# First batch's heads all in fp32, the first head's bias by a matmul with ones, and conversions of two weights ordered by a ramp

## The chip, the cores and the metric

One core of a Trainium2 chip runs the program. The metric is the device time of one execution in microseconds (us). The engines: TensorE (PE; PEld is its weight load), VectorE (DVE), ScalarE (ACT), GpSimd (POOL), and SyncE (SP), whose queue issues every DMA here.

## The reference

```python
# attention: 4 batches, 8 heads, 576 rows, 64 columns
scores = q @ k.T / 8
cum = cumsum(maximum(s, 0))
bias = minimum(-(cum[:, None] - cum[None, :]), 0)
scores = where(causal, -1e9, scores + bias)
attn = exp(scores - max(scores)); attn /= sum(attn) + 1e-9
x = attn @ v                      # heads side by side: 2304 x 512
# two feed-forward parts
c = (x @ w1) * (x @ w2)           # 2304 x 1024
x2 = c @ w3 @ w_out               # 2304 x 512
h = x2 @ w_in                     # 2304 x 2048
out = (h - tanh(h)) @ w_out2      # 2304 x 512
```

The inputs q, k, v and s are fp32. The weights are float64, and the kernel reads their bits.

## The kernel before, in words

The order of the work is not that of the code. Every step is first written down as an operation with its engines, an estimated duration, the buffers that it reads and writes, and a priority (lower goes first). A planner (class `Plan`) then runs a list scheduling over these estimates and emits the instructions in the order that comes out; each engine works through its own list in that order. The numbers of `PARAM` set priorities and costs. Head number n has the priority 100n, products of the first feed-forward part have 1.0e6 and go where TensorE would otherwise wait. Where nothing is there for TensorE in the first 150 us, the planner puts in fillers: matmuls of `msk` into bank 2 (line 499), whose result nobody reads.

A head has five query tiles, 64, 128, 128, 128 and 128 rows, in two groups (tiles 0 to 2, and 3 and 4). For batch 0 the first groups of the eight heads come first (heads 0 to 7 in the numbering), then the second groups (8 to 15), then batch 1 in the same way (16 to 31). For a tile TensorE computes the scores with the bias, `red` on VectorE adds the mask and takes the row's extreme, ScalarE does exp (line 594), TensorE transposes (line 624), the result is copied to SBUF, and `pv` sums V (lines 659, or 661 and 664).

Heads come in two forms. In the full form q, k and the exp are plain fp32: one matmul for the scores (line 577), in which five rows under q and k (tile `rqk`) carry the bias, fetched by DMA from `rel`, the cumulative sums less the one in the middle of each tile; the transposed exp is copied into `en`. In the split form each fp32 operand becomes a high and a low part in a faster format by a copy and a subtraction (`split`): `qs`, `kh`, `kl`, `vs`, `eh`, `el`; the scores are two matmuls (lines 579 and 580), the sum of V two rows of them (661 and 664), and the halves are added on VectorE (line 671). All first groups of batch 0 and the second groups of its heads 0 and 1 are in the full form (`natb=2`), everything later in the split form.

For every pair of heads TensorE transposes the row sums (line 603), VectorE inverts them (604, 605), two DMAs bring them through DRAM into `xr`, and the pair's output is multiplied by it (697) and split into `xh` and `xl` for the products (line 723).

Weights pass through `assemble`: a DMA of the float64 bits, one step on ScalarE (431), four on VectorE (432 to 437), and then a split. For w1 and w2 there are sixteen such conversions of 128x512, eight for each half of the columns, with two priorities for the halves.

Of the kernel before, what the change touches and what calls it, by code (L numbers as in the profile page):

```python
# [16 lines left out]
P = 128  # L17
B, H, S, D = 4, 8, 576, 64
NH = B * H
# [18 lines left out]
PARAM = dict(byf=(0,), dsub=1000.0, dsub0=1000.0, dcopy=1000.0, dcopy0=600.0, dother=1000.0, dother0=1000.0, spi=500.0, lay=6, lay0=4, layp=2.2e5, layf=2.95e5, gate=0, dve0=1000.0, early=100.0e3, raw0=0, rawp=-700.0, ng=3, nosb=2, cut=(1,), convq=1200.0, natb=2, abk=1, wap=0.95e6, dve=1000.0, act=0.0, pool=0.0, sem=160.0, pesem=180.0, slow=1.1, convp=790.0, npre=4,  # L38
# [227 lines left out]
def tile_kernel(ctx, tc, qk, v, s, w1, w2, w3t, w_out, w_in, w_out2, out):  # L266
# [80 lines left out]
    def pe(cost, fn, r, w, prio):  # L347
        pl.op([("PE", cost, fn)], r=r, w=w, prio=prio)
# [114 lines left out]
    def values():  # L463
        m = nc.vector.memset
        m(fix.t[:NH], 1.0)
        m(fix.t[D:D + 5], 1.0)
        for R in rqk:
            m(R.t[D:D + 32, S:], 0.0)
        m(const.t[:, 0:1], SQ_B)
        m(const.t[:, 1:2], -T2)  # L470
        m(ssum.t, 1.0)
        m(msk.t[:, D:], 0.0)
        for e in e2:
            for t in range(5):
                if EW[t] > QT[t][1]:
                    m(e.t[:, EOFF[t] + QT[t][1]:EOFF[t] + EW[t]], 0.0)
            m(e.t[D:, EOFF[0]:EOFF[0] + D], 0.0)
        for x, o in ((eh, EB), (el, EB), (en, 0)):
            m(x.t[D:, o + 1024:].bitcast(F32), 0.0)
    pl.op([("DVE", 2700.0, values)], w=[const, ssum, (msk, 1), eh, el, en, fix] + [(R, 1) for R in rqk] + e2, prio=-2900)  # L480

    def patterns():
        make_identity(nc, ident.t)
        nc.gpsimd.affine_select(fix.t[D:D + 5], fix.t[D:D + 5], [[1, S]], ALU.is_ge, 0.0, D, -P)
        nc.gpsimd.affine_select(fix.t[D:D + 5], fix.t[D:D + 5], [[-1, S]], ALU.is_ge, 0.0, P - 1 - D, P)
        nc.gpsimd.affine_select(msk.t[:, 448:], msk.t[:, 448:], [[-1, P]], ALU.is_ge, MASKED8, 0, 1)
    pl.op([("POOL", 3000.0, patterns)], w=[ident, (fix, 1), (msk, 1)], prio=-2500)
# [19 lines left out]
    dve(lambda: nc.vector.tensor_tensor_scan(rel.t[2 * NH:, :S], fix.t[:NH], rel.t[:NH, :S], 0.0, op0=ALU.mult, op1=ALU.add), S, [(rel, 0), (fix, 0)], [(rel, 5)], -1000)  # L507
# [24 lines left out]
    def head(h, full, groups=(0, 1)):  # L532
        b, hh = divmod(h, H)
        i = n_head[0] % 2
# [10 lines left out]
        if not full:  # L545
            dma(lambda: KL.t[D:D + 10, :qb].bitcast(F32), lambda: kb_d.t[h, :, :, :qb].rearrange("n t s -> (n t) s"), 10 * qb * 4, [kb_d], [(KL, 1)], pr - 245)
        else:
            for t0, t1 in ((0, 3), (3, 5)) if 1 in groups else ((0, 3),):
                a, o = ROFF[t0]
                dma(lambda t0=t0, t1=t1: R.t[D + t0:D + t1, S:S + qb],  # L550
                    lambda t0=t0, t1=t1, a=a: rel.t[a + h:a + h + 1, :(t1 - t0) * S].rearrange("p (t s) -> p t s", s=S)[:, :, :qb],
                    (t1 - t0) * qb * 4, [(rel, range(t0, t1))], [(R, 1)], pr - 245)
# [12 lines left out]
        def softmax_tile(t):  # L565
# [5 lines left out]
            for n, (k0, k1) in enumerate(pieces):  # L571
                bk = s_ring.next()

                def mm(bk=bk, k0=k0, k1=k1):
                    o_ = bk.t[:nq, :k1 - k0]
                    if full:
# [4 lines left out]
                if full:  # L581
                    pe(c_pe4(k1 - k0), mm, [R], [bk], p_)
                else:
                    pe(2 * c_pe(k1 - k0, nq), mm, [Q, Q2, KH, KL], [bk], p_)
# [154 lines left out]
    for half in range(2):  # L739
        for k in range(KC):  # L740
            for src, hb, lb in ((w1, w1h, w1l), (w2, w2h, w2l)):
# [3 lines left out]
                        PARAM["convp"] + half * PARAM["convq"], PARAM["rawp"] if half == 0 and 2 * k + (src is w2) < PARAM["raw0"] else None)  # L745
# [194 lines left out]
```

## Time and profile before

| | us |
|---|---|
| median of 3 runs | 985.87 |
| lowest, highest | 984.68, 987.29 |
| the profiled execution | 984.61 |
| its span | 982.9 |
| TensorE busy in the span | 955.8 |
| VectorE, ScalarE, GpSimd busy | 721.6, 603.7, 400.1 |

The profile is of one execution, and the span is what lies between its first and last instruction. A busy TensorE includes the fillers and the drain of its matmuls. The clock of TensorE is given as a share of 2.4 GHz.

### The profile page before, as it was taken

Reading aid. Unit: us, or ns where it says so; the run is one execution under the profiler, and the core shown is the slowest. Engines: PE = TensorE matmul, PEld = TensorE weight load, DVE = VectorE, ACT = ScalarE, POOL = GpSimd, SP = SyncE. Lnnn points to the kernel's source line nnn. Section 1 sums busy time; section 2 is a strip of 40 time slices with the busy share of each in tenths; the row PEclk is TensorE's granted clock in tenths of the full one; section 3 lists DMA queues with packets and bytes.
Section 4 is the critical chain, followed back from the end, with each engine's and each line's share of the span. In section 5 each row is a group of like instructions: output and inputs, shape, how many; then the busy total and the mean of one; then the engine's idle time right before and its main releaser. Section 6 shows DMA issues by size and latency. Waiting matters only on the chain.

```text
span 982.9 us, 16588 instructions
## 1 busy us (share of the span) xinstructions
PE 955.8 (97%) x5650; PEld 835.4 (85%) x5650; DVE 721.6 (73%) x1449; ACT 603.7 (61%) x1379; POOL 400.1 (41%) x341
## 2 busy tenths in 40 slices
PE   7989799999999999999999999999999999999998
PEld 6568699999999999888988898878888888888897
DVE  7879998788988959996786988985445455454454
ACT  4777867788878854443454447665455555654565
POOL 2346675654554434442254637442222222222222
PEclk7999899999999999999999999999999999999999
DMA  5667537645545315558679773103003000200010
GB/s 171 186 192 229 146 86 234 190 138 174 162 140 181 103 39 160 179 166 277 203 269 325 247 245 141 44 26 125 1 1 107 22 1 1 87 1 0 1 44 22
DMA packets 70092, 124.45 MB, mean 127 GB/s; under 512 B 6780, under 2 KB 39172, under 8 KB 70008
## 3 DMA queue, kind: packets, MB, share of 16 engines
q1 hardware_dynamic: 70008, 123.41, 39.3%
q8 instruction: 44, 0.72, 0.3%
q14 instruction: 40, 0.33, 0.1%
HBM read 93.34 MB, written 25.99 MB: 121 GB/s over the span
## 4 chain that ended last, share of the span: by engine, by line
PE 82%; DVE 7%; DMA 5%; issue 2%; ACT 2%; POOL 1%; SPq 0%; DVEq 0%; POOLq 0%; ACTq 0%
PE bank L865 19%; PE bank L723 16%; PE bank L888 6%; PE bank L886 6%; PE bank L887 6%; PE bank L624 4%; PE bank L828 3%; PE bank L827 3%; PE bank L829 3%; PE bank L661 2%; PE bank L664 2%; PE bank L579 2%; PE bank L580 2%; DMA xr<-r_d 2%; PE bank L791 1%
## 5 line engine op out<-in xcount | busy, mean ns | idle before, releaser
L334 POOL TENSOR_TENSOR gl<-pg,gh 128x512 fp32r<-128x512 f32 (+1 forms) x78 | 98.0, 1257 | 261.4 <-ACT gh L328 230.0
L865 PE MATMUL bank<-x2b,wih 128*128 128x512 f32 (+1 forms) x640 | 182.4, 370 | 0.0
L876 DVE TENSOR_TENSOR pg<-bank,u 128x512 f32<-128x512 f32 (+1 forms) x80 | 50.8, 635 | 142.3 <-ACT th L875 140.4
L865 PEld LDWEIGHTS bank<-x2b,wih 128*128 128x128 f32 x640 | 116.7, 188 | 21.7
L865 PE MATMUL bank<-x2b,wil 128*128 128x512 f32 (+1 forms) x320 | 117.9, 368 | 0.0
L888 PE MATMUL bank<-voh,gl 128*128 128x512 f32 x288 | 113.1, 393 | 0.4 <-POOL gl L334 0.3
L886 PE MATMUL bank<-voh,gh 128*128 128x512 f32 x288 | 113.0, 392 | 0.2 <-ACT gh L328 0.2
L887 PE MATMUL bank<-vol,gh 128*128 128x512 f32 x288 | 112.6, 391 | 0.0
L328 ACT ACTIVATE gh<-pg 128x512 fp32r<-128x512 f32 (+1 forms) x80 | 47.1, 589 | 87.2 <-DVE pg L880 85.7
L594 ACT ACTIVATE e<-e,nmx 64x64 f32<-64x64 f32 (+4 forms) x160 | 88.7, 556 | 12.3 <-DVE nmx L588 11.5
L873 ACT ACTIVATE u<-bank 128x512 f32<-128x512 f32 (+1 forms) x80 | 44.3, 554 | 71.4 <-PE bank L865 65.5
L431 ACT ACTIVATE wt<-wraw 128x512 f32<-128x512 f32 x72 | 47.9, 671 | 60.1 <-DMA wraw<-w_out 17.0
L624 PE MATMUL bank<-ident,e 128*128 128x128 f32 (+1 forms) x480 | 80.8, 277 | 3.4 <-ACT e L594 1.4
L723 PE MATMUL bank<-xh,w2h 128*128 128x288 f32 x256 | 80.6, 315 | 1.4 <-DVE cst L731 1.4
L723 PE MATMUL bank<-xh,w1h 128*128 128x288 f32 x256 | 81.3, 318 | 0.6 <-ACT asb L328 0.3
L588 DVE CUSTOM_DVE_ANT_0 e<-bank,msk 64x64 f32<-64x64 f32 (+4 forms) x160 | 64.6, 416 | 20.1 <-PE bank L580 9.1
L723 PE MATMUL bank<-xl,w2h 128*128 128x288 f32 x256 | 75.7, 296 | 0.0
L723 PE MATMUL bank<-xh,w1l 128*128 128x288 f32 x256 | 75.7, 296 | 0.0
L723 PE MATMUL bank<-xl,w1h 128*128 128x288 f32 x256 | 75.6, 295 | 0.0
L723 PE MATMUL bank<-xh,w2l 128*128 128x288 f32 x256 | 75.5, 295 | 0.0
L332 DVE TENSOR_TENSOR el<-bank,eh 128x512 fp32r<-128x512 f32 (+2 forms) x162 | 73.5, 474 | 2.5 <-ACT eh L328 2.0
L880 DVE COPY_PREDICATED pg<-mk,th 128x512 f32<-128x512 uint32 (+1 forms) x80 | 61.6, 770 | 12.5 <-ACT mk L878 5.1
(139 smaller groups left out, 2629.2 us busy)
## 6 DMA issues: line engine op xcount, KB each, us to landing
rqk<-qk SPq DMA_DIRECT2D x30, 576.0 KB
wraw<-w_out SPq DMA_DIRECT2D x24, 512.0 KB
c_d<-cst SPq DMA_DIRECT2D x32, 288.0 KB
wraw<-w SPq DMA_DIRECT2D x16, 512.0 KB
wraw<-w3t SPq DMA_DIRECT2D x16, 512.0 KB
cf<-c_d SPq DMA_DIRECT2D x32, 256.0 KB
wraw<-w_in SPq DMA_DIRECT2D x16, 512.0 KB
x_d<-x2s SPq DMA_DIRECT2D x16, 512.0 KB
```

The source lines that it names most:

```text
L332: o = [("DVE", c_dve(n), lambda: nc.vector.tensor_tensor(dst(), a(), b().bitcast(F32), op=ALU.subtract))]
L334: o.append(("POOL", c_pool2(n), lambda: nc.gpsimd.tensor_tensor(dst(), a(), b().bitcast(F32), op=ALU.subtract)))
L588: nc.vector.tensor_tensor_reduce(e.t[:nq, EOFF[t] + k0:EOFF[t] + k1], bk.t[:nq, :k1 - k0], bi.t[:nq, bo + k0:bo + k1], -0.125, 3.0e38 if f ...
L594: act(lambda: nc.scalar.activation(et(), et(), AF.Exp, bias=nmx.t[:nq, i, tm:tm + 1], scale=-1.0, accum_out=ssum.t[:nq, pj, t, i:i + 1]), ...
L624: nc.tensor.transpose(bk.t[:rows, n * P:(n + 1) * P], e.t[:, EOFF[t] + c * P:EOFF[t] + c * P + rows], ident.t)
L723: nc.tensor.matmul(bk.t[:, :HALF], w_.t[:, k, f * P:(f + 1) * P], x_.t[:, k, o:o + HALF], start=k == 0 and j == 0, stop=k == KC - 1 and j ...
L865: nc.tensor.matmul(bk.t[:, :w], w_.t[:, k, a], X2.t[:, i, k, :w], start=k == 0 and n == 0, stop=k == KC - 1 and n == 2)
L876: dve(lambda u=u, pg=pg, hp=hp, c_=c_: nc.vector.tensor_tensor(c_(pg), hp(), c_(u), op=ALU.mult), w, [bk, u], [pg], pr)
L880: dve(lambda pg=pg, mk=mk, th=th, c_=c_: nc.vector.copy_predicated(c_(pg), c_(mk).bitcast(U32), c_(th)), w, [mk, th], [pg], pr, two=True)
L886: nc.tensor.matmul(bank[n].t, gh.t[:, a], voh[f].t, start=f == 0, stop=False)
L887: nc.tensor.matmul(bank[n].t, gh.t[:, a], vol[f].t, start=False, stop=False)
L888: nc.tensor.matmul(bank[n].t, gl.t[:, a], voh[f].t, start=False, stop=f == NF2 - 1)
```

## The change

Three things are changed. First, `natb` goes from 2 to 8: the second groups of heads 2 to 7 of batch 0 take the full form too, and the pool with the second set of split buffers opens after all of them. Second, the very first group (head 0, tiles 0 to 2) takes its bias from `rel` by a second matmul, whose other operand, in unused columns of the second exp buffer, has a first row of ones and zeros below; its rows of the bias in `rqk` are no longer fetched. The constants are set in two steps, with those that the first heads need ahead of the scan, the others behind the row blocks, and GpSimd's patterns are three operations. Third, the priorities of the sixteen conversions: 790 for the first eight and 1990 for the others become ramps from 590 to 940 and from 1790 to 2140 in steps of 50 (`convp` 790 to 590, new `ramp0` and `ramp1` of 50.0). The table `PARAM` is left out below.

```diff
--- before.py
+++ after.py
...
@@ -465,9 +465,14 @@
         m(fix.t[:NH], 1.0)
         m(fix.t[D:D + 5], 1.0)
         for R in rqk:
-            m(R.t[D:D + 32, S:], 0.0)
-        m(const.t[:, 0:1], SQ_B)
-        m(const.t[:, 1:2], -T2)
+            m(R.t[D:D + 5, S:], 0.0)
+        m(sel(), 0.0)
+        m(sel()[0:1], 1.0)
+    sel = lambda: e2[1].t[:NH, EOFF[4]:EOFF[4] + P]
+    pl.op([("DVE", 2600.0, values)], w=[fix, (e2[1], 4)] + [(R, 1) for R in rqk], prio=-2900)
+
+    def more():
+        m = nc.vector.memset
         m(ssum.t, 1.0)
         m(msk.t[:, D:], 0.0)
         for e in e2:
@@ -475,16 +480,18 @@
                 if EW[t] > QT[t][1]:
                     m(e.t[:, EOFF[t] + QT[t][1]:EOFF[t] + EW[t]], 0.0)
             m(e.t[D:, EOFF[0]:EOFF[0] + D], 0.0)
+        m(const.t[:, 0:1], SQ_B)
+        m(const.t[:, 1:2], -T2)
         for x, o in ((eh, EB), (el, EB), (en, 0)):
             m(x.t[D:, o + 1024:].bitcast(F32), 0.0)
-    pl.op([("DVE", 2700.0, values)], w=[const, ssum, (msk, 1), eh, el, en, fix] + [(R, 1) for R in rqk] + e2, prio=-2900)
+    pl.op([("DVE", 1900.0, more)], w=[const, ssum, (msk, 1), eh, el, en] + [(e, range(4)) for e in e2], prio=-850)
 
     def patterns():
-        make_identity(nc, ident.t)
         nc.gpsimd.affine_select(fix.t[D:D + 5], fix.t[D:D + 5], [[1, S]], ALU.is_ge, 0.0, D, -P)
         nc.gpsimd.affine_select(fix.t[D:D + 5], fix.t[D:D + 5], [[-1, S]], ALU.is_ge, 0.0, P - 1 - D, P)
-        nc.gpsimd.affine_select(msk.t[:, 448:], msk.t[:, 448:], [[-1, P]], ALU.is_ge, MASKED8, 0, 1)
-    pl.op([("POOL", 3000.0, patterns)], w=[ident, (fix, 1), (msk, 1)], prio=-2500)
+    pl.op([("POOL", 1700.0, lambda: make_identity(nc, ident.t))], w=[ident], prio=-2600)
+    pl.op([("POOL", 1330.0, patterns)], w=[(fix, 1)], prio=-2500)
+    pl.op([("POOL", 400.0, lambda: nc.gpsimd.affine_select(msk.t[:, 448:], msk.t[:, 448:], [[-1, P]], ALU.is_ge, MASKED8, 0, 1))], w=[(msk, 1)], prio=-2400)
 
 
     def constants(i):
@@ -504,7 +511,7 @@
         dma(lambda i=i: rqk[i].t[D:D + 5, :S], lambda: fix.t[D:D + 5], 5 * S * 4, [(fix, 1)], [(rqk[i], 1)], -990)
     dma(lambda: rel.t[:NH, :S], lambda: s, NH * S * 4, [], [(rel, 0)], -1000)
     dve(lambda: nc.vector.tensor_scalar(rel.t[:NH, :S], rel.t[:NH, :S], 0.0, 8.0, op0=ALU.max, op1=ALU.mult), S, [(rel, 0)], [(rel, 0)], -1000, fast=True)
-    dve(lambda: nc.vector.tensor_tensor_scan(rel.t[2 * NH:, :S], fix.t[:NH], rel.t[:NH, :S], 0.0, op0=ALU.mult, op1=ALU.add), S, [(rel, 0), (fix, 0)], [(rel, 5)], -1000)
+    dve(lambda: nc.vector.tensor_tensor_scan(rel.t[2 * NH:, :S], fix.t[:NH], rel.t[:NH, :S], 0.0, op0=ALU.mult, op1=ALU.add), S, [(rel, 0), (fix, 0)], [(rel, 5)], -1000, extra=650.0)
 
 
     for t, (q0, q1) in enumerate(QT):
@@ -531,6 +538,7 @@
 
     def head(h, full, groups=(0, 1)):
         b, hh = divmod(h, H)
+        one = n_head[0] == 0
         i = n_head[0] % 2
         pj = n_head[0] // 2 % 2
         pr = n_head[0] * 100.0
@@ -544,7 +552,7 @@
             lambda: qk[h, :rows].rearrange("p (two s) -> p two s", two=2)[:, :, :qb], rows * 2 * qb * 4, [], [(R, 0)] if full else [R], pr - 250)
         if not full:
             dma(lambda: KL.t[D:D + 10, :qb].bitcast(F32), lambda: kb_d.t[h, :, :, :qb].rearrange("n t s -> (n t) s"), 10 * qb * 4, [kb_d], [(KL, 1)], pr - 245)
-        else:
+        elif n_head[0] > 1:
             for t0, t1 in ((0, 3), (3, 5)) if 1 in groups else ((0, 3),):
                 a, o = ROFF[t0]
                 dma(lambda t0=t0, t1=t1: R.t[D + t0:D + t1, S:S + qb],
@@ -573,12 +581,18 @@
 
                 def mm(bk=bk, k0=k0, k1=k1):
                     o_ = bk.t[:nq, :k1 - k0]
-                    if full:
+                    if one:
+                        a, o = ROFF[t]
+                        nc.tensor.matmul(o_, rq()[:D, q0:q1], rk()[:D, k0:k1], start=True, stop=False)
+                        nc.tensor.matmul(o_, sel()[:, :nq], rel.t[a:a + NH, o + k0:o + k1], start=False, stop=True)
+                    elif full:
                         nc.tensor.matmul(o_, rq()[:D + 5, q0:q1], rk()[:D + 5, k0:k1], start=True, stop=True)
                     else:
                         nc.tensor.matmul(o_, Q.t[:, q0:q1], KH.t[:, k0:k1], start=True, stop=False)
                         nc.tensor.matmul(o_, Q2.t[:NR, q0:q1], KL.t[:NR, k0:k1], start=False, stop=True)
-                if full:
+                if one:
+                    pe(2 * c_pe4(k1 - k0), mm, [(R, 0), (rel, t), (e2[1], 4)], [bk], p_)
+                elif full:
                     pe(c_pe4(k1 - k0), mm, [R], [bk], p_)
                 else:
                     pe(2 * c_pe(k1 - k0, nq), mm, [Q, Q2, KH, KL], [bk], p_)
@@ -742,7 +756,7 @@
                 convert(src[k * P:(k + 1) * P, half * 512:(half + 1) * 512],
                         lambda hb=hb, k=k, half=half: hb.t[:, k, half * 512:(half + 1) * 512], (hb, k * 2 + half),
                         lambda lb=lb, k=k, half=half: lb.t[:, k, half * 512:(half + 1) * 512], (lb, k * 2 + half),
-                        PARAM["convp"] + half * PARAM["convq"], PARAM["rawp"] if half == 0 and 2 * k + (src is w2) < PARAM["raw0"] else None)
+                        PARAM["convp"] + half * PARAM["convq"] + (2 * k + (src is w2)) * PARAM["ramp%d" % half], PARAM["rawp"] if half == 0 and 2 * k + (src is w2) < PARAM["raw0"] else None)
     raw_r.bufs, raw_r.i = raw, 0
     for h in range(H + 1):
         if h == PARAM["natb"]:
```

The places where the new order matters follow. VectorE's list at the start, before (the memset of `msk` and `fix` and of both `rqk` stand ahead; `rel` holds the cumulative sums):

```order
L471 MEMSET ssum 128x20
L472 MEMSET msk 128x512
L476 MEMSET e_115 128x64 x4
L477 MEMSET e_115 64x64
L476 MEMSET e_116 128x64 x4
L477 MEMSET e_116 64x64
L479 MEMSET eh 64x128
L479 MEMSET el 64x128
L479 MEMSET en 64x128
L506 TENSOR_SCALAR rel<-rel 32x576
L507 SCALAR_TENSOR_TENSOR rel<-fix,rel 32x576
L513 TENSOR_SCALAR rel<-rel 32x576 x5
```

and of the change, from the memset of `fix`:

```order
L466 MEMSET fix 5x576
L468 MEMSET rqk_105 5x576
L468 MEMSET rqk_106 5x576
L469 MEMSET e_116 32x128
L470 MEMSET e_116 1x128
L513 TENSOR_SCALAR rel<-rel 32x576
L514 SCALAR_TENSOR_TENSOR rel<-fix,rel 32x576
L520 TENSOR_SCALAR rel<-rel 32x576 x3
L476 MEMSET ssum 128x20
L477 MEMSET msk 128x512
```

The relu, the scan and three of the five row blocks now stand behind six short rows; the other memsets follow them.

TensorE's list in the second groups of batch 0, before, from the sum of V of head 2 on (`bank_60` takes the sum, `e` is the exp, `eh` and `el` its parts):

```order
L661 MATMUL bank_60<-eh,vs_114 128x256 x4
L661 MATMUL bank_60<-eh,vs_114 128x128
L664 MATMUL bank_60<-el,vs_114 64x256 x4
L664 MATMUL bank_60<-el,vs_114 64x128
L579 MATMUL bank_59<-kh_794,qs_793 128x288
L580 MATMUL bank_59<-kl_795,q_796 128x288
L624 MATMUL bank_61<-ident,e_116 128x128 x4
L579 MATMUL bank_58<-kh_111,qs_110 128x448
L580 MATMUL bank_58<-kl_112,q_113 128x448
```

and of the change, from the sum of V of head 0's second group on:

```order
L673 MATMUL bank_60<-en,rv_108 64x256 x4
L673 MATMUL bank_60<-en,rv_108 64x128
L638 MATMUL bank_63<-ident,e_116 128x128 x4
L737 MATMUL bank_65<-xh_89,w2h 128x288
L737 MATMUL bank_65<-xl_91,w2h 128x288
L737 MATMUL bank_65<-xh_89,w2l 128x288
L589 MATMUL bank_58<-rqk_105 128x448
L617 MATMUL bank_62<-ident,ssum 4x128
L638 MATMUL bank_61<-ident,e_116 128x128 x4
L589 MATMUL bank_59<-rqk_105 128x288
```

Each pair of split matmuls is one fp32 matmul now, for the scores and for the sum of V; products stand between them.

VectorE's list in the same part of the program, before:

```order
L329 CAST kh_111<-rqk_105 128x576
L332 TENSOR_TENSOR el<-bank_62,eh 128x4x128
L437 SCALAR_TENSOR_TENSOR wt_82<-wraw_81,wt_82 128x512
L731 TENSOR_TENSOR cst_131<-bank_65,asb_133 128x288
L332 TENSOR_TENSOR el<-bank_63,eh 64x128
L588 ISA e_116,nmx<-bank_59,msk 128x448
L588 ISA nmx 128x1
```

and of the change:

```order
L437 SCALAR_TENSOR_TENSOR wt_83<-wraw_107,wt_83 128x512
L329 CAST w1h<-wt_83 128x512
L432 TENSOR_SCALAR wt_88<-wt_88 128x512
L433 TENSOR_SCALAR wt_88<-wt_88 128x512
L435 SCALAR_TENSOR_TENSOR wt_88<-wraw_87,wt_88 128x512
L602 ISA e_116,nmx<-bank_59,msk 128x448
L602 ISA nmx 128x1
L602 ISA e_116,nmx<-bank_58,msk 128x288
```

The casts of k and the subtractions of `el` are gone, and steps of conversions stand between the reductions.

## Rows read from the trace of the kernel before

**Rows 1.** Busy time of each engine by stretch, TensorE's clock, DMA.

```profile
core 0: us, PE busy (x) PEld busy (x) DVE busy (x) ACT busy (x) POOL busy (x), PEclk, DMA share, GB/s
...
13.00:50.40 37.40, 35.63 (x193) 23.13 (x194) 29.09 (x86) 25.74 (x87) 12.57 (x12) 0.89 0.58 162
50.40:105.80 55.40, 46.95 (x353) 40.11 (x351) 47.66 (x112) 41.38 (x104) 31.78 (x34) 1.00 0.67 208
105.80:140.00 34.20, 31.75 (x230) 29.99 (x231) 31.91 (x79) 24.93 (x76) 23.98 (x26) 0.90 0.42 118
140.00:240.00 100.00, 99.78 (x790) 97.95 (x790) 83.06 (x238) 80.74 (x224) 53.37 (x55) 1.00 0.60 183
...
```

**Rows 2.** The same stretches, the fillers of line 499 alone.

```profile
13.00:50.40 37.40, 6.05 (x47) 4.91 (x47) 0.89 0.58 162
50.40:105.80 55.40, 5.44 (x58) 3.72 (x58) 1.00 0.67 208
105.80:140.00 34.20, 1.56 (x13) 0.92 (x13) 0.90 0.42 118
```

**Rows 3.** TensorE alone, in stretches of 2 us; the clock stands behind its count.

```profile
10.00:12.00 2.00, 0.00 (x0) 0.77 0.76 276
12.00:14.00 2.00, 0.98 (x4) 0.50 0.57 134
20.00:22.00 2.00, 2.00 (x9) 0.67 0.00 0
106.00:108.00 2.00, 1.25 (x8) 0.67 0.92 273
112.00:114.00 2.00, 2.00 (x12) 0.63 0.42 94
```

**Rows 4.** TensorE's timeline: start, time, line, operands, wait ahead with what ended it.

```profile
1.05 7.27 PE L499 MATMUL bank<-msk 128*128 128x128 bf16 x100 [1.05 <-DVE msk L495]
13.02 1.38 PE L577 MATMUL bank<-rqk 69*64 69x64 f32 x4 [4.69 <-DMA rqk<-rel]
...
48.83 1.40 PE L659 MATMUL bank<-en,rv 128*64 128x320 f32 x6 [0.65 <-ACT en L328]
...
50.43 0.27 PE L603 MATMUL bank<-ident,ssum 128*6 128x128 f32 x1
...
105.31 0.27 PE L603 MATMUL bank<-ident,ssum 128*4 128x128 f32 x1 [2.84 <-DVE el L332]
```

**Rows 5.** TensorE's timeline: scores and sums of V, in fp32 and split.

```profile
47.18 0.99 PE L577 MATMUL bank<-rqk 69*128 69x448 f32 x2
...
61.74 2.16 PE L659 MATMUL bank<-en,rv 128*64 128x256 f32 x10
...
100.76 0.77 PE L661 MATMUL bank<-eh,vs 128*128 128x256 f32 x5
101.37 0.69 PE L664 MATMUL bank<-el,vs 128*64 128x256 f32 x5
```

**Rows 6.** Timeline of VectorE and of SP's queue at the start.

```profile
2.35 1.15 DVE L468 MEMSET rqk<- 32x576 f32 x2
...
5.65 0.45 DVE L506 TENSOR_SCALAR rel<-rel 32x576 f32<-32x576 f32 x1
...
6.13 1.35 DVE L507 TENSOR_TENSOR_SCAN rel<-fix,rel 32x576 f32<-32x576 f32 x1
...
7.52 2.34 DVE L513 TENSOR_SCALAR rel<-rel 32x576 f32<-32x576 f32 x5
...
8.91 1.44 SPq L325 DMA_DIRECT2D rqk<-rel  x2
```

**Rows 7.** VectorE's groups by shape, 0 to 140 us: busy, mean ns, idle before.

```profile
L437 DVE SCALAR_TENSOR_TENSOR wt<-wraw,wt 128x512 uint32<-128x512 uint32 x16 | 14.1, 884 | 0.1
...
L332 DVE TENSOR_TENSOR el<-bank,eh 128x512 fp32r<-128x512 f32 x12 | 7.8, 680 | 0.4 <-ACT eh L328 0.4
...
L332 DVE TENSOR_TENSOR vs<-rv,vs 128x320 fp32r<-128x320 f32 x1 | 2.5, 2533 | 0.0
```

More of the change, by code (lines that the diff above doesn't have):

```diff
@@ L37 @@
 NR = D + 10
-PARAM = dict(byf=(0,), dsub=1000.0, dsub0=1000.0, dcopy=1000.0, dcopy0=600.0, dother=1000.0, dother0=1000.0, spi=500.0, lay=6, lay0=4, layp=2.2e5, layf=2.95e5, gate=0, dve0=1000.0, early=100.0e3, raw0=0, rawp=-700.0, ng=3, nosb=2, cut=(1,), convq=1200.0, natb=2, abk=1, wap=0.95e6, dve=1000.0, act=0.0, pool=0.0, sem=160.0, pesem=180.0, slow=1.1, convp=790.0, npre=4,
+PARAM = dict(ramp0=50.0, ramp1=50.0, byf=(0,), dsub=1000.0, dsub0=1000.0, dcopy=1000.0, dcopy0=600.0, dother=1000.0, dother0=1000.0, spi=500.0, lay=6, lay0=4, layp=2.2e5, layf=2.95e5, gate=0, dve0=1000.0, early=100.0e3, raw0=0, rawp=-700.0, ng=3, nosb=2, cut=(1,), convq=1200.0, natb=8, abk=1, wap=0.95e6, dve=1000.0, act=0.0, pool=0.0, sem=160.0, pesem=180.0, slow=1.1, convp=590.0, npre=4,
              nbias=3, keep=0.5, ff=0.0, fu=150.0e3, wlast=8, bw=370.0, ntr=3, actb=1, actn=0, spp=-80.0, ne=2, nsb=2, ncf=5, outlag=15)
```

## The prediction

> **What bounds the kernel now.** I read the profile from the end backwards. The table by stretches [rows 1] shows TensorE busy for 99.78 of the 100 us after 140 us. The stretches before it are another matter, so whatever the change is worth is decided ahead of 140 us: there I split TensorE's time into work and loss. Loss is idle time, the fillers on `msk` (matmuls whose result nobody reads) [rows 2], and half of the time in which TensorE works at the lower of its two clocks (1.2 instead of 2.4 GHz) [rows 3].
>
> - A, 0 to 13.0 us: 100 fillers, then a wait of 4.69 us until the first scores start at 13.02, ended by the DMA that writes rows of `rel` into `rqk` [rows 4]. All 13.0 us are loss.
> - B, 13.0 to 50.4, the first query groups of batch 0, up to the fourth transposition of row sums at 50.43 [rows 4]: 35.63 busy, less 6.05 of fillers, less about 4.2 because the clock is at its lower level from 11.1 to 21.3 us [rows 3]: 25.4 of work, 12.0 lost.
> - C, 50.4 to 105.8, the second query groups, up to the eighth such transposition at 105.31 [rows 4]: 46.95 less 5.44 makes 41.5 of work, 13.9 lost. VectorE is the busiest engine here, 47.66 of 55.4 us, a share of 0.86 [rows 1].
> - D, 105.8 to 140, the start of batch 1: 31.75 less 1.56, less about 3.4 for a lower clock from 106.7 to 113.5 [rows 3]: 26.8 of work, 7.4 lost.
>
> Together 46.3 us are lost. From then on TensorE has no gap worth naming, so the end is 984.61 (the profiled execution, 1.26 under the median of 985.87) less the loss that goes, plus the TensorE work that comes. Stages after 140 us get the same matmuls in nearly the same order, and I let them cancel.
>
> **The change part by part.**
>
> *TensorE work added.* Six heads of batch 0 now do their second group in full fp32. For the weighted sum of V the trace has both forms: five chunks, 1152 columns, take 2.16 us in fp32; split, 100.76 to 102.06, 1.30 us [rows 5]. That is 0.86 us more, 0.75 ns a column. The scores are 448 + 288 + 288 = 1024 columns, at the same rate 0.77 us more. Six heads: 9.8 us. The first head's bias by ones is a second fp32 matmul over 64 + 192 + 320 = 576 columns; at 2.16 us per 1152 columns, 1.1 us. Sum +10.9 us. From below the same numbers without the drain of the last matmul, from above the fp32 score row, 0.99 us for 448 columns [rows 5], 2.2 ns a column against 0.56: 10 to 14. I take 10.9, the nearer row in length.
>
> *Start (A).* The first head no longer waits for `rel` to pass through the DMA; its bias is read from `rel` by a matmul. On VectorE the order puts the memsets of `rqk` at the same place, ending 2.35 + 1.15 = 3.5 us [rows 6]; two small ones follow and then relu, scan and the first row block, where seventeen other memsets stood in between. 3.8 + 0.45 + 1.35 + 0.5 gives 6.1, against 8.0 before [rows 6], and the first matmul starts at about 6.3 if `s` has landed by 3.8; it has by 5.65, where relu ran without a wait for it, which makes 8.1 the other bound. Head 1 still goes through the DMA: issue at 8.91 and use at 13.02 are 4.1 us apart [rows 4, 6]. Three row blocks are done by 7.1, SP has one weight load fewer ahead, so the issue comes at 7.3 to 8.2 and head 1 at 11.4 to 12.5. Head 0's scores (2.2 us with the ones) and transposes lie inside that wait. I take 5 us less loss; from 2 (the late `s`, head 1 hardly earlier) to 6.5.
>
> *B.* The same instructions in other order, conversions a little later (six first steps on VectorE instead of eight before the fourth sums), and 74 fillers, beside the 28 in the wait for head 1, instead of 47 after the first scores. Fillers go where TensorE would wait, so they cost little: 0; from -1.5 to +2.7, the latter being 27 more fillers at the lower clock's 0.1 us each.
>
> *C.* Between the fourth and the eighth transposition VectorE loses its 19 subtractions (0.68 us for the common one [rows 7]), 4 casts and 4 additions, about 16 us, and gets five more conversions of four steps (a step is up to 0.88 us [rows 7]), 15 us. So VectorE stays near 47 while fourteen of the sixteen conversions are finished by the eighth transposition instead of twelve; ScalarE loses the copies that fed the splits, GpSimd the subtractions of q, k and v, and SP the 128-row loads, the `kb_d` reads and the copies of q. TensorE gets 9.8 us and gives 45 product matmuls away (57 instead of 102), 288 columns at the split rate, 0.14 us each, 6.3 us, which are done after C and are not lost. Its work becomes 45.0. The unknown is how well it can be packed: at VectorE's share of today, 0.86, C lasts 52.3 and loses 7.3; at TensorE's share of D, 31.75 of 34.2, 48.5 and 3.5; with all waits as they are, 13.9. I take 5.8, nearer to the first two, because the largest single wait there, 2.84 us, ends with a subtraction that no longer exists [rows 4].
>
> *D.* The lower clock from 106.7 follows that 2.84 us gap. With the gap gone I take 2 of the 3.4 us back, and 1.7 from VectorE, which starts one conversion here instead of four: 3.7 lost instead of 7.4; from 2 to 7.4. The buffers that odd heads of batch 1 need now open only when the last fp32 head is through; 48 products stand in TensorE's order between the eighth transposition and the first such head, and hide it.
>
> *The ramp.* It spreads the first eight conversions over heads 6 to 9 and the others over heads 18 to 21. It adds no instruction; its cost is in the counts used for B and C.
>
> One rule bears on this. Where VectorE and GpSimd overlap, the trace shows a 320-column subtraction in SBUF taking 2.53 us, while a 512-column one that reads PSUM takes 0.68 [rows 7]. The Trainium skill (SBUF — State Buffer, "SBUF: two separate sides") says that the two engines share one port pair as an exclusive lock, held for a whole instruction. By that rule GpSimd's lost subtractions would also shorten the conversions on VectorE, and C would pack as in the better bound.
>
> **Sum.** Loss 8.0 + 12.0 + 5.8 + 3.7 = 29.5 instead of 46.3: 16.8 less. Work +10.9. Net -5.9: 985.87 - 5.9 = 980.0 us.
>
> **Rivals.**
>
> 1. *TensorE takes VectorE's place and the waits stay.* Within a head the chain scores, reduction, exp, transposition, copy into `en`, sum of V is serial, and `en` has one buffer: the trace has a matmul on `en` that waited 0.65 us for ScalarE's copy [rows 4]. If that chain, now with fp32 matmuls in it, holds C at 13.9 and D at 7.4, only A gains: -5 + 10.9 = +5.9, 991.8. It decides where C and D together lose more than 15.4 us (break-even with A at 8; today 21.3, forecast 9.5), and the result is slower by over 0.3% beyond 18.4. For it: no filler or product stands in most of C's new order. Against it: the waits seen today in C end with subtractions and split loads that go.
> 2. *The start is only rearranged.* Only 30 fillers stand before the first scores and 28 after the second tile; while TensorE waited 4.69 us the clock fell, and it came back at 21.3 only [rows 3, 4]. If head 1 starts near 12.5 and the lower clock lasts some 5 us longer, A saves 2 and B loses 2.8 more: -2 + 2.8 - 8.1 - 3.7 + 10.9 = -0.1, 985.8. The Trainium skill (TensorE: Matmul & The Clock Gate, "HAM oscillation — how this bites in real kernels") says that idle gaps between bursts send the clock back to its lower level each time; the trace agrees, with 0.50 at 12 to 14 us after the gap of 4.69 us.
> 3. *Everything packs better.* C at 3.5, D at 2, A at 6.5: 24.0 instead of 46.3, -22.3 + 10.9 = -11.4, 974.5. The lock above would work this way. Against it: ScalarE, at 41.38 of 55.4 us in C [rows 1], is little relieved.
>
> **How the numbers follow.** Forecast 0.46, rival 1 0.15, rival 2 0.19, rival 3 0.20. A measurement of this kernel can tell about 0.3% (3 us) from no change. The forecast and rival 3 are faster by more, 0.66; rival 2 is within, 0.19; rival 1 is slower, 0.15. The likeliest time is 980.0. The low end takes all of rival 3 and what the bounds of A and B leave beyond it, 970; the high end reaches rival 1, 992. With the forecast alone the range would be 975 to 984.
>
> **What would show it.** First scores at 6 to 8 us and head 1 at 11.4 to 12.5; the fourth transposition of sums at about 45 us and the eighth near 96; a share of TensorE's busy time above 0.9 in that stretch with hardly any fillers; no lower clock at batch 1's start. The forecast is wrong if the eighth transposition comes after 102 us, or if TensorE shows new gaps after 140 us, which I let cancel.

## The result and the profile after

The changed kernel takes 976.95 us (median of 4 runs, 975.06 to 980.52) beside 986.58 of the kernel before: a ratio of 0.9894, 95% interval 0.9853 to 0.9935. In eight later runs beside 27 of before it was 980.57 us (974.85 to 982.94), 0.9922 with 0.9893 to 0.9951. So it is faster by 7.7 to 10.5 us by the ratios (6.5 to 9.6 by the medians). The forecast of 980.0 us, 5.9 less, had its sign right and was a little too small. One execution of all those reported here, 3314.4 us of the kernel without fillers, is left out as an outlier.

The table by stretches again, on the same events as [rows 1]: the fourth and the eighth transposition of sums end the second and the third stretch.

```profile
core 0: us, PE busy (x) PEld busy (x) DVE busy (x) ACT busy (x) POOL busy (x), PEclk, DMA share, GB/s
0.00:13.00 13.00, 10.59 (x69) 8.08 (x69) 9.28 (x36) 4.86 (x9) 3.92 (x11) 1.00 0.65 208
13.00:46.20 33.20, 31.44 (x219) 21.77 (x219) 26.25 (x74) 25.25 (x86) 12.59 (x12) 1.00 0.60 175
46.20:97.10 50.90, 50.34 (x299) 36.35 (x297) 44.76 (x103) 38.20 (x92) 23.23 (x23) 1.00 0.63 182
97.10:140.00 42.90, 40.79 (x320) 38.16 (x318) 31.83 (x96) 28.52 (x98) 25.08 (x31) 1.00 0.49 142
140.00:240.00 100.00, 99.44 (x792) 97.74 (x791) 86.38 (x245) 84.97 (x232) 55.21 (x58) 1.00 0.58 179
```

The fillers alone (line 506 now) in the same stretches, as [rows 2]:

```profile
0.00:13.00 13.00, 6.55 (x58) 6.02 (x58) 1.00 0.65 208
13.00:46.20 33.20, 7.24 (x74) 5.27 (x74) 1.00 0.60 175
46.20:97.10 50.90, 2.95 (x36) 2.43 (x36) 1.00 0.63 182
97.10:140.00 42.90, 1.46 (x12) 0.81 (x12) 1.00 0.49 142
```

In stretch C TensorE is busy for 50.34 of 50.90 us, 0.99, where it was 46.95 of 55.40 [rows 1]. Its lost time there is 0.56 idle and 2.95 of fillers: 3.5 us instead of 13.9. VectorE, the busiest engine before, stands at 0.88 behind it. The waits of TensorE from 46.2 to 140 us say the same; the 2.84 us of [rows 4] is gone, the longest is 1.1 and the three others that are listed are 0.5 each:

```profile
engine line waited for: us in total, times, longest us
PE bank L592 <- DMA r_d<-rinv: 1.1, 1, 1.1
```

TensorE's timeline at the start and at the three transpositions that mark the stretches, to be read beside [rows 4]:

```profile
1.05 3.38 PE L506 MATMUL bank<-msk 128*128 128x128 bf16 x30 [1.05 <-DVE msk L502]
4.46 0.47 PE L586 MATMUL bank<-rqk 64*64 64x64 f32 x2
6.26 0.47 PE L587 MATMUL bank<-rel,e 32*64 32x64 f32 x2 [1.34 <-DVE rel L520]
...
8.54 3.17 PE L506 MATMUL bank<-msk 128*128 128x128 bf16 x28
11.63 1.43 PE L586 MATMUL bank<-rqk 64*128 64x320 f32 x2
12.99 0.80 PE L587 MATMUL bank<-rel,e 32*128 32x320 f32 x2
...
14.56 0.85 PE L589 MATMUL bank<-rqk 69*64 69x64 f32 x4
...
20.65 0.27 PE L617 MATMUL bank<-ident,ssum 128*6 128x128 f32 x1
...
46.18 0.27 PE L617 MATMUL bank<-ident,ssum 128*6 128x128 f32 x1
...
97.11 0.27 PE L617 MATMUL bank<-ident,ssum 128*4 128x128 f32 x1
```

One thing here doesn't fit the clock column. The column reads 1.00 all through. Yet the 28 fillers from 8.54 us take 3.17 us, 0.113 us each, and line 587's matmul over 320 columns at 12.99 takes 0.80 us, while line 586's over the same 320 columns, 1.4 us earlier, takes 1.43. The instructions show TensorE at its lower level, 1.2 GHz, until about 13 us; the column doesn't. Up to there TensorE works 10.59 - 6.55 = 4.04 us beside the fillers, and half of it, 2.0 us, is loss that the column misses. In what follows the column is used where it shows a fall, and the lengths of equal instructions where it doesn't.

### The profile page after: what moved, and what is told of

The parts are those of the page before. It is cut to its first block, busy times and chain, and to the rows that moved or that the text cites. A ratio compares the mean times of both kernels' runs of the same rounds, so it can differ in the third digit from the quotient of the medians.

```text
span 973.3 us, 16442 instructions
## 1 busy us (share of the span) xinstructions
PE 958.5 (98%) x5619; PEld 832.9 (86%) x5619; DVE 699.6 (72%) x1421; ACT 597.6 (61%) x1360; POOL 384.2 (39%) x330
## 4 chain that ended last, share of the span: by engine, by line
PE 89%; DVE 4%; DMA 3%; issue 2%; ACT 1%; POOL 1%; SPq 0%; DVEq 0%; ACTq 0%; POOLq 0%
PE bank L879 19%; PE bank L737 18%; PE bank L902 6%; PE bank L900 6%; PE bank L901 6%; PE bank L638 5%; PE bank L842 3%; PE bank L841 3%; PE bank L843 3%; PE bank L673 3%; PE bank L589 2%; PE bank L675 2%; PE bank L678 2%; PE bank L592 2%; PE bank L591 2%
## 5 line engine op out<-in xcount | busy, mean ns | idle before, releaser
L638 PE MATMUL bank<-ident,e 128*128 128x128 f32 (+1 forms) x480 | 78.5, 274 | 0.2
L894 DVE COPY_PREDICATED pg<-mk,th 128x512 f32<-128x512 uint32 (+1 forms) x80 | 62.6, 783 | 13.6 <-ACT mk L892 5.7
L879 PEld LDWEIGHTS bank<-x2b,wil 128*128 128x128 f32 x320 | 60.3, 188 | 10.5
```

Of the source, the lines that this page charges most:

```text
L638: nc.tensor.transpose(bk.t[:rows, n * P:(n + 1) * P], e.t[:, EOFF[t] + c * P:EOFF[t] + c * P + rows], ident.t)
L879: nc.tensor.matmul(bk.t[:, :w], w_.t[:, k, a], X2.t[:, i, k, :w], start=k == 0 and n == 0, stop=k == KC - 1 and n == 2)
L894: dve(lambda pg=pg, mk=mk, th=th, c_=c_: nc.vector.copy_predicated(c_(pg), c_(mk).bitcast(U32), c_(th)), w, [mk, th], [pg], pr, two=True)
```

## The experiments

The first theory: relieved of the split heads' products, VectorE, ScalarE and GpSimd let TensorE pack from 50 to 140 us; the ones give the start; the ramp matters little. The first rival: the new order of the conversions and the start carry the gain, and the fp32 heads only cost their work.

The account of the runs that leave out a part, made nearly as the prediction made it: idle time, plus fillers, plus half of the time that the clock column shows at the lower level. Idle time at the lower level is counted in both terms here, which adds at most 1.3 us to a row. It is of one execution each. All in us; the ratio is to the kernel before, each beside its own runs.

| kernel | ratio (95%) | lost to 4th | 4th to 8th | 8th to 150 us | sum |
|---|---|---|---|---|---|
| before | 1 | 25.9 | 13.6 | 7.9 | 47.3 |
| changed | 0.9894 (0.9853-0.9935) | 18.0 | 3.5 | 3.8 | 25.3 |
| changed, again | 0.9922 (0.9893-0.9951) | 19.1 | 3.2 | 5.9 | 28.2 |
| ramp and ones, 2 fp32 heads | 1.0004 (0.9978-1.0029) | 19.2 | 14.4 | 14.0 | 47.6 |
| ramp and ones, 5 fp32 heads | 0.9965 (0.9942-0.9988) | 18.7 | 8.5 | 6.3 | 33.6 |
| fp32 heads alone | 0.9996 (0.9973-1.0018) | 24.1 | 4.5 | 9.0 | 37.5 |
| ramp and fp32 heads, no ones | 0.9986 (0.9964-1.0009) | 27.0 | 3.7 | 8.3 | 38.9 |
| ones and fp32 heads, no ramp | 1.0043 (1.0018-1.0068) | 25.3 | 13.9 | 1.9 | 41.1 |
| the same, early flat order | 1.0018 (0.9991-1.0044) | 30.4 | 3.1 | 5.9 | 39.4 |

Where the ones are in, the column misses lower clock at the start (not in the run without the ramp): by the lengths of equal instructions it lasts to about 13 us in the changed kernel and to 19.5 or so in the others, an estimated 2 to 4 us of loss more than the table shows.

**Two fp32 heads, with ramp and ones.** As before, only the first two heads of batch 0 have their second groups in full fp32.

```diff
-convq=1200.0, natb=8, abk=1
+convq=1200.0, natb=2, abk=1
```

> The changed kernel with full fp32 only in the first two heads of the first batch, as before; the new conversion order and the ones for the first head's bias stay. The first theory (VectorE, ScalarE and GpSimd, relieved of the split heads' products, let TensorE pack from 50 to 140 us): only the start is gained, the stretch from the 4th to the 8th transposition of the sums is again about 55 us long with about 14 us lost, the stretch to the 12th 34 us; time about 982, 0.9955 of the kernel before. The rival (conversion order and start carry the gain, the six heads only cost their roughly 10 us of extra matmul work): faster than the changed kernel, about 968 us, 0.981.

Measured: 988.59 us (12 runs, 985.49 to 993.16), 1.0004. The stretch from the fourth to the eighth transposition and its fillers:

```profile
50.10:104.90 54.80, 49.94 (x352) 41.47 (x350) 45.09 (x110) 38.51 (x93) 29.98 (x31) 0.94 0.63 193
50.10:104.90 54.80, 6.21 (x65) 4.46 (x64) 0.94 0.63 193
```

Length and loss are what the first theory said, 54.8 and 14.4 us (3.3 of them for the clock, at 0.94 on the mean). The rival's 968 us is 20 us off. The time missed the theory by 6 us as well: the start of batch 1 lost 14.0 us (7.9 before), and the fourth transposition comes at 50.1 us (50.4 before).

**Five fp32 heads.** The same line with `natb=5`.

> The changed kernel with five heads of the first batch in full fp32 in place of eight (two before); the ramp and the ones stay. If the gain comes head by head (each head in fp32 takes its splits, products and reloads off VectorE, ScalarE and GpSimd for 1.6 us of TensorE): half of the 8 us between two heads (1.0004 of before) and eight (0.992), 983 to 985 us, 0.996. If what counts is that no split head is left among the first batch's (its products are then all to be fitted in, and TensorE waits in the second stretch as before): nothing is gained, 986 to 989 us, 1.000, with 12 us or more lost between the 4th and the 8th transposition of the sums. If three heads fewer save 4.9 us of work without losing the packing: 976 us, 0.988.

Measured: 985.24 us (12 runs), 0.9965: between two heads and eight.

```profile
49.30:104.60 55.30, 53.06 (x369) 42.02 (x368) 48.85 (x110) 41.69 (x101) 27.56 (x27) 1.00 0.65 197
49.30:104.60 55.30, 6.23 (x78) 5.02 (x79) 1.00 0.65 197
```

It lost 8.5 us there. With 14.4 at two heads and 3.5 at eight that is 1.7 to 2.0 us of loss taken away per head, for an estimated 1.6 us of extra matmul work. The gain comes head by head. Most of what is left of it stands at the start of batch 1, where 14.0, 6.3 and 3.8 us are lost.

**All heads in fp32, nothing else.** The kernel before with `natb=8`.

> The kernel before with all eight heads of the first batch in full fp32, conversions in their old order, the first head's bias by its DMA rows. First theory: the lost TensorE time between 50 and 140 us falls from 21 us to 7 to 10 us, the work grows by about 9.5 us, time 980 to 984, about 0.995 of before. The rival: nothing is gained but the work is paid, about 995 us, 1.010.

Measured: 988.1 us (12 runs), 0.9996. The stretch and its fillers (line 499, the old numbering):

```profile
48.90:101.90 53.00, 50.89 (x303) 37.54 (x301) 44.08 (x103) 37.73 (x88) 22.55 (x21) 1.00 0.55 157
48.90:101.90 53.00, 2.34 (x30) 1.93 (x30) 1.00 0.55 157
```

The loss does go (4.5 instead of 13.6) with neither ramp nor ones, so the fp32 heads do it. The account is 9.8 lower. The work (TensorE's busy time in the whole span, less fillers and half of that at the lower clock) goes from 928.2 to 937.6, 9.4 more, and the time stays. Neither theory's time came out; the mechanism is the first's, and no net gain shows. The start of batch 1 gained nothing by the heads: 9.0 lost, 7.9 before.

**No ones.**

```diff
-        one = n_head[0] == 0
+        one = False
-        elif n_head[0] > 1:
+        else:
```

> The changed kernel, but the first head's bias comes by the DMA rows as the other heads' does. Theory: head 0 scores wait for the DMA's landing, head 1 comes 2 to 4 us later, and since TensorE is the bound from there on, that stays to the end: 979 to 981 us, 3 us over the changed kernel. Rival (the start is made up later, as TensorE catches up with what waits there): the same as the changed kernel, 976 to 977 us.

Measured: 986.76 us (12 runs), 0.9986, 6 to 10 us over the changed kernel: two to three times what the theory gave to the ones. TensorE's timeline at the start:

```profile
11.66 1.38 PE L589 MATMUL bank<-rqk 69*64 69x64 f32 x4 [4.26 <-DMA rqk<-rel]
...
24.91 0.27 PE L617 MATMUL bank<-ident,ssum 128*6 128x128 f32 x1
```

And the first and the last stretch of 2 us with a lower clock there (length, TensorE's busy time and count, clock, DMA share, GB/s):

```profile
10.00:12.00 2.00, 0.34 (x2) 0.70 0.43 130
24.00:26.00 2.00, 2.00 (x11) 0.89 0.11 24
```

The wait for the bias rows is back, 4.26 us, and from 10.8 to 24.4 us the clock is at its lower level.

**No ones, the wait filled.** 75 fillers more behind the 86th, in the order of the kernel without ones.

```diff
+            if o.fn is self.filler:
+                n += 1
+                for _ in range(75 if n == 86 else 0):
+                    self.filler()
```

> The changed kernel without the ones (the first head's bias by DMA rows again), with 75 more filler matmuls in the wait for those rows from 7.4 us on. Clock theory (the ones gain by leaving no wait after which the clock falls): the 13.6 us at the lower clock from 10 us on go, 6 to 7 us are gained against the same kernel without these fillers, about 980 us, 0.992. The rival (the earlier scores are what the ones gain): as without the fillers, 986 to 987 us, 0.9986.

Measured: 983.79 us (12 runs), 0.9977, 0.9956 to 0.9999. The first sums (line 623 here):

```profile
1.05 11.60 PE L512 MATMUL bank<-msk 128*128 128x128 bf16 x161 [1.05 <-DVE msk L508]
...
20.51 0.27 PE L623 MATMUL bank<-ident,ssum 128*6 128x128 f32 x1
```

They come at 20.51, 4.4 us earlier than without the fillers and as early as in the changed kernel, although head 0's scores still start only at 12.58. In this profile the clock alone brings back the start that the ones give. Over the runs the difference is 0.9 us by the ratios and 3.0 by the medians, and the intervals overlap, so a gain of the clock alone isn't shown; the profiled pair, 987.6 and 980.9 us of span, is wider apart than the medians. Neither theory's time came out: about 5 us to the changed kernel are left, and 7.6 us are lost at the start of batch 1, where the changed kernel loses 3.8.

**No ramp.**

```diff
-PARAM = dict(ramp0=50.0, ramp1=50.0, ... convp=590.0,
+PARAM = dict(ramp0=0.0, ramp1=0.0, ... convp=790.0,
```

> The changed kernel, but with the conversions' priorities as before (all behind the heads by one flat number, no ramp). Theory: the relief of VectorE by the fp32 heads is what matters, the order of the conversions little: within 3 us of the changed kernel, 976 to 980 us, though the 4th transposition of the sums comes earlier and the stretch to the 8th is longer. Rival (the mixing is what lets TensorE pack): most of the gain is gone, 983 us or more.

Measured: 991.47 us (12 runs), 1.0043. The rival was right. The first two products in TensorE's timeline:

```profile
58.33 0.60 PE L737 MATMUL bank<-xh,w1h 128*128 128x288 f32 x1 [4.29 <-ACT xh L328]
59.88 0.61 PE L737 MATMUL bank<-xl,w1h 128*128 128x288 f32 x1 [0.96 <-POOL xl L334]
```

And its clock: one stretch at the start, then the first and the last below 1.00 behind these products:

```profile
20.00:22.00 2.00, 2.00 (x9) 0.50 0.18 49
...
58.00:60.00 2.00, 0.71 (x2) 0.59 0.38 68
68.00:70.00 2.00, 2.00 (x13) 0.85 0.00 0
```

A product stands in TensorE's list before its `xh` is made, and everything behind it waits 4.29 us; then the clock is low from 58.3 to 68.5 us. With half of that time the two waits make 10.4 us, as much as the 10.4 more that are lost between the fourth and the eighth transposition. In the changed kernel the first products start at 35.5 us without a wait. But the clock was also low from 14 to 27 us in this execution, ahead of all products, and 7.3 us more were lost up to the fourth transposition than in the changed kernel's table row. This execution, 997.85 us, is at the slow end of its runs, so its account is larger than the medians' difference.

**Early, but flat.** `ramp0=0.0, ramp1=0.0` alone, `convp=590.0` kept.

> The changed kernel with the conversions' priority at its new, earlier value but flat, without the ramp that mixes them one by one with the heads. If what matters of the new order is that the conversions start among the first heads: within 3 us of the changed kernel, 977 to 983 us, 0.992. If it is the spacing by the ramp: as with the old flat value, 988 to 992 us, 1.003.

Measured: 989.31 us (12 runs), 1.0018. The spacing matters, not only the earlier level; only one spacing, steps of 50, was tried. It has the same wait in another place of TensorE's timeline, with lower clock in parts of 46 to 61 us:

```profile
46.11 0.40 PE L737 MATMUL bank<-xh,w1h 128*128 128x288 f32 x1 [3.50 <-ACT xh L328]
```

**The changed kernel again.**

> The changed kernel once more, beside the others and in more runs, since none of its parts alone showed its gain. If the gain is the changed program's own: 0.989 of the kernel before within 0.003, about 977 us beside 988. If it was an accident of a few runs in which TensorE's clock happened not to fall: the mean granted clock is spread from 0.985 to 0.999 over the runs, and the ratio comes out at 0.993 to 0.998.

Measured: 0.9922. The whole interval is below 1, so the gain is the program's own. Its size isn't settled: 0.9922 lies between the two forecasts, and the interval reaches into both. Two rows to be read beside those of the changed kernel above, of the same program:

```profile
12.99 1.43 PE L587 MATMUL bank<-rel,e 32*128 32x320 f32 x2
...
23.48 0.27 PE L617 MATMUL bank<-ident,ssum 128*6 128x128 f32 x1
```

Both executions have the same matmul at 12.99; the one takes 0.80 us and reaches its first sums at 20.65, the other takes 1.43 and reaches them at 23.48. In the second, TensorE is at its lower level until about 19.5 us. That is 2.83 us of the spread from 974.85 to 982.94; this execution is the slowest of the second set and the one above the fastest of the first.

**Without the 28 fillers.** They are left out where the changed kernel's order is issued.

```diff
+                if 30 <= n <= 57:
+                    continue
```

> The changed kernel in its own order, with the 28 filler matmuls left out that stand between the second and the third score tile of head 0 and held TensorE from 8.54 to 11.71 us. Theory of the start: head 0's third tile and head 1 come 2 to 3 us earlier and TensorE is the bound from there on: 974 to 975 us, 0.9870. The rival (TensorE reaches its higher clock only after it has been busy, so the fillers' 3.2 us are given back as a longer stretch at the lower clock, or head 1's rows land too late): the same as the changed kernel, 976 to 979 us, or 3 us slower where the clock rises later still.

Measured: 980.48 us (8 runs), 0.9932 (0.9907 to 0.9956): the same as the changed kernel. TensorE at head 0's third tile:

```profile
10.53 1.43 PE L592 MATMUL bank<-rqk 64*128 64x320 f32 x2 [1.94 <-DVE nmx L608]
```

That is the third tile (line 592 here) in TensorE's timeline. It comes 1.1 us earlier and then waits for VectorE's reduction of the first tile, which stands behind the last memsets in VectorE's list. The fillers weren't what held head 1, whose scores come at 14.75 (14.56 and 15.85 in the two executions of the changed kernel).

**Fillers in the first head's wait.**

```diff
+                        for _ in range(12 if t == 0 else 0):
+                            pl.filler()
```

> The changed kernel in its own order with 12 more filler matmuls between head 0's first score matmul and its ones matmul, where TensorE stood idle for 1.33 us at 4.9 us, at the lower clock (fillers take 113 ns there up to 11.7 us; in the kernel before, without a wait in that place, they take 45 to 54 ns from 4 us on). Theory (that idle time keeps the clock low until 13 or 19.5 us): the clock rises at 4 to 8 us, the first transposition of the sums comes at 18 to 19 us in place of 20.7 to 23.5, and with TensorE the bound from there 2 to 5 us are gained, 975 to 978 us, 0.988 beside 0.992. The rival (the reductions on VectorE or the DMA of head 1's rows set the start): fillers run faster, the scores wait, the same as the changed kernel, 980 us.

Measured: 979.57 us (6 runs), 0.9906 (0.9876 to 0.9936). That is the lowest ratio beside the changed kernel's own, and not to be told from it. The fillers, the ones matmul behind them (line 589 here) and the third tile in TensorE's timeline:

```profile
4.79 1.06 PE L506 MATMUL bank<-msk 128*128 128x128 bf16 x12
6.26 0.32 PE L589 MATMUL bank<-rel,e 32*64 32x64 f32 x2 [0.42 <-DVE rel L520]
...
10.54 0.80 PE L586 MATMUL bank<-rqk 64*128 64x320 f32 x2 [1.25 <-DVE nmx L604]
```

Its clock later on, again first and last stretch:

```profile
12.00:14.00 2.00, 1.51 (x11) 0.53 0.90 290
18.00:20.00 2.00, 2.00 (x8) 0.77 0.00 0
```

The clock rose by 6.3 us as foreseen (0.32 us where the same matmul took 0.47), but TensorE then had to wait 1.25 us for the reduction, and from 12.1 to 18.5 us the clock was at its lower level, about as long as it had been won. The mechanism held; no gain shows.

**Fillers in the waits of the kernel before.** 95 behind its 100th filler, 45 ahead of the eighth transposition of sums.

> The kernel before, its order unchanged, with filler matmuls (which compute nothing that is used) in the two waits after which its clock falls: 95 more from 8.3 us on while head 0 waits for its bias, and 45 before the 8th transposition of the sums, where TensorE stands 2.8 us at 103 us. Clock theory (a good part of what the changed kernel gains is that TensorE isn't idle long enough for its clock to fall): the 17 us at the lower clock go, TensorE is busy for most of them, so 6 to 8.6 us are gained, about 980 us, 0.992. The rival (the waits themselves are what costs, the clock falls only where TensorE has slack): 986 to 989 us, 1.000.

Measured: 987.99 us (12 runs), 0.9998 (0.9969 to 1.0027). This doesn't settle the price of the clock, as the fillers moved the waits. Two rows of TensorE's timeline:

```profile
21.09 0.30 PE L584 MATMUL bank<-rqk 69*64 69x64 f32 x2 [1.43 <-DMA rqk<-qk]
...
106.06 3.98 PE L505 MATMUL bank<-msk 128*128 128x128 bf16 x45 [2.12 <-DVE xf L683]
```

With the start at the higher clock TensorE ran into a DMA at 21 us and the clock fell there (0.50 from 22 to 24 us). The 45 fillers waited 2.12 us themselves, by the row for a step on VectorE, then took 3.98 us with the clock low for part of it.

**No fillers at all.** The changed kernel's order without the planner's fillers.

> The changed kernel in its own order without any filler matmul that the planner put into waits (204 of them with 18.6 us in the profiled run). Clock theory: waits of some 10 us in the first 50 us and 4 us after it are now idle, the clock stays or falls low there, the work of the first 46 us (25 us at full speed) takes up to twice as long: 985 to 996 us, 0.998 to 1.009. The rival (fillers only pass the time, or stand in the way of work that has come ready): 978 to 981 us, 0.992.

Measured: 981.7 us (8 runs), 0.9925 (0.9897 to 0.9952). The rival's number: this interval and that of the changed kernel cover each other. Its profile does show the first sums at 23.74 at the lower clock, and the fourth at 54.7 us instead of 46.2 to 49.5, but that execution is at the slow end of its runs.

## Why the prediction was right, and where it was not

*C* was right in place and cause. Forecast 5.8 lost, with 48.5 us and 3.5 lost as the better bound; it came out at 3.5 and 50.9 us, with 47.4 us of work for the 45.0 forecast. Two, five and eight fp32 heads lose 14.4, 8.5 and 3.5, which shows that the heads do it. By which of the engines they relieve isn't shown: no run takes VectorE's subtractions, ScalarE's copies, GpSimd's subtractions or the loads away one at a time, and VectorE's share in C is 0.88 now, where it was 0.86. The eighth transposition came at 97.1 for "near 96".

*The work added* is paid in full. With the heads alone, 9.8 us less loss and 9.4 more work leave the time unchanged. The prediction's C, D and heads' work, -8.1, -3.7 and +9.8, a net gain of 2.0, stands against -0.4 us measured (0.9996, -2.7 to +1.8). No saving of the heads by themselves beyond their price is shown, and 2.0 is not excluded; D's 3.7 did not come with them.

*The lock.* The four forms of conversion steps on VectorE, from 0 to 140 us, before (the first is that of [rows 7]):

```profile
L437 DVE SCALAR_TENSOR_TENSOR wt<-wraw,wt 128x512 uint32<-128x512 uint32 x16 | 14.1, 884 | 0.1
L435 DVE SCALAR_TENSOR_TENSOR wt<-wraw,wt 128x512 uint32<-128x512 uint32 x16 | 14.0, 881 | 0.0
L432 DVE TENSOR_SCALAR wt<-wt 128x512 f32<-128x512 f32 x16 | 11.7, 731 | 0.1
L433 DVE TENSOR_SCALAR wt<-wt 128x512 uint32<-128x512 uint32 x16 | 8.8, 554 | 0.1
```

and now:

```profile
L437 DVE SCALAR_TENSOR_TENSOR wt<-wraw,wt 128x512 uint32<-128x512 uint32 x16 | 13.7, 856 | 0.3
L435 DVE SCALAR_TENSOR_TENSOR wt<-wraw,wt 128x512 uint32<-128x512 uint32 x16 | 13.2, 822 | 0.1
L433 DVE TENSOR_SCALAR wt<-wt 128x512 uint32<-128x512 uint32 x16 | 12.6, 786 | 0.3
L432 DVE TENSOR_SCALAR wt<-wt 128x512 f32<-128x512 f32 x16 | 9.7, 604 | 0.0
```

They sum to 49.2 us, against 48.6 before: three forms are shorter, line 433 is longer. By the rule of the Trainium skill ("SBUF — State Buffer", "SBUF: two separate sides") they should have shortened with GpSimd's subtractions gone; in the sum no shortening shows. Step by step the trace agrees with the rule. A step of line 433 with GpSimd idle beside it takes 0.41 to 0.43 us in both kernels; the one below, beside a subtraction of GpSimd, takes 1.43:

```profile
11.40 3.98 POOL L334 TENSOR_TENSOR el<-rel,eh 32x576 fp32r<-32x576 f32 x2 [3.34 <-ACT eh L524]
14.25 1.43 DVE L433 TENSOR_SCALAR wt<-wt 128x512 uint32<-128x512 uint32 x1
```

Of the 64 steps, 38 overlapped an instruction of GpSimd before (0.92 us on the mean, 0.53 for the others) and 37 do now (0.92 and 0.56). In C GpSimd's subtractions of q, k and v went from 20 to 2, but those of the weights (`w1l`, `w2l`) from 4 to 10. That the steps would meet GpSimd less often is what failed. With the heads alone 28 overlap, and the four forms sum to 40.3 us.

*A and B.* Head 0's first scores get their bias at 6.26 (their first matmul, which needs none, starts at 4.46) and the fourth transposition comes at 46.2, for "6 to 8" and "about 45". By the account with 2.0 us for the clock that the column misses, 20.0 us were lost for the 20.0 forecast. That is luck: it is the faster of two profiled executions (49.5 in the other), and the way to it was another. But head 1 came at 14.56 (15.85 in the other execution), not 11.4 to 12.5. The step that failed is that the DMA's landing would set it: head 1's scores show no wait. The runs put two things in its place. The third tile of head 0, which stands ahead of them, can't start before 10.53, because it waits for a reduction that VectorE starts at 10.26 us, behind its memsets and the last row blocks (in the changed kernel itself the 28 fillers hold it until 11.63). And everything up to 13 or 19.5 us goes at the lower clock. So a piece of rival 2 came true. The Trainium skill (TensorE: Matmul & The Clock Gate, "HAM oscillation — how this bites in real kernels") has idle gaps between bursts send the clock back each time; the two rows of the run with 12 fillers agree, low again from 12 us after a gap of 1.25 us, while a gap of 1.1 us in the changed kernel, at 137.85 us in batch 1, left no mark in the column. Which gaps do it these runs don't show.

*D* lost 3.6 us up to 140 for the 3.7 forecast in the profiled execution. In the other, split scores at 141.77 us waited 2.3 us for a DMA and the clock fell behind them, so the prediction's 2 us given back hold only in some runs.

*The ramp* is the term that was mis-sized. The prediction said that it adds no instruction and that its cost lies in the counts, and let the rest of the order follow. Without it the time goes from 0.992 to 1.0043 or 1.0018 of before: 9 to 12 us, more than the whole gain. Mechanism seen: in both flat orders a product of line 737 stands ahead of its `xh`, TensorE waits 4.29 or 3.50 us, and the clock falls behind it. No run moves that product alone, so its share of the 9 to 12 us isn't shown. I read the order for how many products and conversions stand in a stretch and not for whether the operand of the first is there in time.

*The parts don't add.* Heads alone -0.4, heads and ramp -1.4, heads and ones +4, ramp and ones 0, all three -7.7 to -10.5 us. The ramp alone and the ones alone were not run. The forecast's sum came near because it was made on the order of all three together; as a price list of the parts it was wrong. Where the ramp is missing, the products' wait accounts for the stretch that it stands in, but not for the start. Where the ones are missing, the account has the 4.26 us wait, 13.6 us at the lower clock and 4.5 us more in batch 1's start, of which only the clock was tried by itself. The account of the profiled pair closes: 27.3 lost (25.3 and the 2.0) instead of 47.3 and 10.9 of work give -9.1, 0.7 less is idle after 150 us, and the spans differ by 9.6. With the other execution, 28.2 and an estimated 3.8, it gives -4.4, 0.8 more idle after 150 us, and the spans differ by 1.7: it closes to 2 us. Of the rivals, the first (the waits stay) fell with C; the third had C right, but not A.

*The end.* After 140 us the changed kernel has 99.44 of 100 busy against 99.78 [rows 1], no new gap, as promised.

## What to carry to other kernels

Where one engine is nearly full, add up its lost time by stretch and price a change against the new order as a whole: here the heads alone and each pair of parts were worth nothing, and all three together 8 us. The account suggests a reason, that a part left out opens one lull and the clock falls behind it; it isn't shown by itself, and the run without fillers, with lulls and a fall of its clock, kept its gain. In a list that is issued in order, look at the first instruction of each kind that is pulled forward and ask whether its operand exists by then; one product a few us too early stood beside a loss of 9 to 12 us here. Doing a split step in full precision on the full engine paid its price and showed no more, and became a gain only with the other two parts.

## What the runs showed of the hardware

- The clock column reads 1.00 at the start where instructions run at the lower level: fillers of 0.113 us at 8.5 us, against 45 to 54 ns each in the kernel before from 4 us on (19 to 22 in each microsecond).
- The same program leaves the lower level at about 13.0 us in one execution and 19.5 in another, by the lengths of equal matmuls (0.80 and 1.43 us at 12.99). What decides between them was not found.
- Keeping TensorE busy with fillers paid little: with none of the planner's, 0.9925; with them, 0.9922; with 12 more at the start, 0.9906, all within each other's intervals. In two of the three profiles with fillers added to an order (12 at the start, 140 in the kernel before) the clock fell again at the next wait.
- A conversion step on VectorE takes longer beside an instruction of GpSimd: over the 64 steps of four forms 0.92 us on the mean in both kernels, and 0.53 and 0.56 without one. For line 433 alone it is 0.41 to 0.43 without, and up to 1.8 beside one.
